# Dense products in half-array pairs, and one value phase per eight score steps, in an attention and gated-MLP block

## The chip, the cores and the metric

The kernel runs on one core of one Trainium2 chip. The metric is the device time of one execution in microseconds (us). TensorE (PE) multiplies, VectorE (DVE) and ScalarE (ACT) read its results from PSUM, GpSimd (POOL) works on SBUF alone, and SyncE (SP) issues nearly all DMA transfers. PEld is TensorE's loading of weights, which overlaps PE.

## The reference

One layer-normalised input of 2048 rows and 512 columns feeds two branches, attention with 32 heads of 16 and a gated MLP with a spatial product over the rows; both are added to the input. Everything is in fp32.

```python
def _A_ref(x, wqkv, wo):                     # attention, H = 32, Dh = 16
    q, k, v = ...                            # x @ wqkv, split by heads
    scores = jnp.einsum("bhqd,bhkd->bhqk", q, k) * (Dh ** -0.5)
    p = _softmax(scores, axis=-1)
    o = jnp.einsum("bhqk,bhkd->bhqd", p, v)
    return o.transpose(...).reshape(B, S, D) @ wo
def _B_ref(x, w_in, w_sp, b_sp, w_out):      # gated MLP, Fh = 896
    z = _gelu(jnp.einsum("bsd,df->bsf", x, w_in))
    z1, z2 = z[..., :Fh], _layernorm(z[..., Fh:], axis=-1)
    g = jnp.einsum("ts,bsf->btf", w_sp, z2) + b_sp[None, :, None]
    return jnp.einsum("bsf,fd->bsd", z1 * g, w_out)
xn = _layernorm(x, axis=-1)
return x + _A_ref(xn, A_wqkv, A_wo) + _B_ref(xn, B_w_in, B_w_sp, B_b_sp, B_w_out)
```

## The kernel before

**Attention.** Heads go in 16 pairs. A *score step* `scores(n)` (L840) makes one tile `st` of 128 keys by 512 queries for both heads of a pair: two matmuls of 50 rows (three parts of 16 and two rows that carry the negative maximum), one on the upper and one on the lower half of the array, into the two banks of one PSUM pair. There are 1024 steps. ACT takes the exponential of the whole pair into a buffer `pf` (L57). A *maximum step* `max_mm(m)` (L572) makes the same scores turned round, queries on partitions, again as two half-array matmuls (48 rows), and DVE reduces them (L580); there are 1024 of these too, and they run `LEAD` = 27 steps ahead. After every 16th, `max_fin` makes the row of maxima, which goes through DRAM into the two extra rows of `qst`. The *value products* `pv` (L814) take two `pf` buffers (two tiles of keys, two heads): four matmuls of 128 rows and 32 columns side by side, in fp32, which the chip does as two instructions each. They add up over 16 steps in the bank `o`, which ACT copies out. Three PSUM pairs (`s`) serve scores and maxima, one bank `o` the values and one bank `d` the dense products.

**Dense work.** All other products go through `mm3` (L167 to L169): both factors are split into a high and a low part, and three matmuls of 128 rows and up to 512 columns add up in the bank `d`. In this order: queries and keys of the later heads (`qk_rest`), the MLP's second half (`z2_all`) with its normalisation (`z2_norm`, mostly on POOL), its first half (`z1_all`), the spatial product (`spatial`, tile name `sp`), `mlp_out` (`mo`) and `attn_out` (`ao`). Each is a generator that yields after every three matmuls. Tiles finished in `d` are copied or added out by ACT or DVE; the splitting into high and low parts follows in generators of `side` and `bg`.

**Order.** The schedule is written out by hand when the kernel is built: the instructions of each engine stand in a fixed order, and semaphores do the rest. The main loop goes through *halves*, two for every three score steps. In an even half PE gets a score, a maximum, a score and then up to four half rounds of value products (`pv_some`); in an odd half a maximum, a score, a maximum and then dense work, as much as a credit allows that spreads it evenly up to step `DENSE` = 925. `later` and `flush` put DMA issues off by so many halves, and `prepare` brings weights in, through three buffers `raw` and POOL (L192, L193). Large tiles come from a ring of `RING` = 20 buffers: in the spatial stage 16 of them hold weights `wsp` and four hold pieces `zs` of z2, read back from DRAM at 512 KB each.

**Before the main loop** a prologue loads and normalises x, turns it round (`turn_x`), and makes queries and keys of the first group of heads (`qk_group(0, ...)`) and all values (`v_tile`).

Of the kernel before, what the change touches and what calls it, by code (L numbers as in the profile page):

```python
# [31 lines left out]
RING = 20  # L32
LEAD = 27
PF = 6
DENSE = 925
HALF = 2.7


@with_exitstack
def fused_block(ctx, tc, x, wqkv, wo, w_in, w_spT, b_sp, w_out, out):  # L40
# [5 lines left out]
    at = ctx.enter_context(tc.tile_pool(name="att", bufs=1))  # L46
# [6 lines left out]
    load = {"A": 0.0, "D": 0.0}  # L53

    def act(out, in_, func, n, **kw):
        load["A"] += 0.16 + n / 1400.0
        return nc.scalar.activation(out, in_, func, **kw)  # L57

    def dve(n, rate=1):
        load["D"] += 0.065 + n / (960.0 * rate)  # L60
        return nc.vector
# [35 lines left out]

    steady = []
    side = []
    left = [0]  # L100
# [6 lines left out]

    late = []  # L110
    now = [-2 * LEAD // 3 - 1]
# [3 lines left out]
    pool = [-1000.0]  # L115

    def clock():
        return HALF * now[0]

    def gps(us):  # L120
        pool[0] = max(pool[0], clock()) + us
        return nc.gpsimd

    def pool_done():
        t = pool[0]
        yield
        while clock() < t:
            yield

    def later(k, fn, *args):  # L130
        late.append((now[0] + k, fn, args))

    def flush():
        due = [l for l in late if l[0] <= now[0]]
        late[:] = [l for l in late if l[0] > now[0]]
        for _, fn, args in due:
            fn(*args)

    def store(dst, src, k=1):
        if steady:  # L140
            later(k, move, dst, src)
        else:
            nc.gpsimd.dma_start(raw(dst), raw(src))

    def piece(nm):
        return big.tile([P, 2, 512], F32R, tag="big", name=nm, bufs=RING)
# [7 lines left out]
    def dpsum(nm, tag="d", n=1):  # L154
        left[0] = n
        return ps.tile([P, 512], F32, tag=tag, name=nm, bufs=1)

    def spsum(nm):

        return ps.tile([P, 2, 512], F32, tag="s", name=nm, bufs=3)  # L160

    def split(dst_h, dst_l, src, n):
        act(dst_h, src, AF.Copy, n)
        dve(n).tensor_sub(dst_l, src, dst_h.bitcast(F32))
# [5 lines left out]

    rawfree = [-1000.0] * 3
# [24 lines left out]
    def prepare(out, loads, freed=None):  # L196


        loads, flight, made = list(loads), [], []
        while loads or flight or made:  # L200
            if made and clock() >= made[0][0]:
                _, k, t = made.pop(0)
                out[k] = t
            if flight and now[0] >= flight[0][0]:
                _, k, l = flight.pop(0)
                t = end(l)
                made.append((pool[0], k, t))
                rawfree.append(pool[0])
            if loads and len(rawfree) > 0 and clock() >= rawfree[0] and (freed is None or freed and now[0] >= freed[0]):
                rawfree.pop(0)  # L210
                if freed:
                    freed.pop(0)
                k, *a = loads.pop(0)
                flight.append((now[0] + 2, k, begin(*a)))
            yield

    wq, w2, w1, wsp, wout, wo_ = {}, {}, {}, {}, {}, {}
    bg = []
# [5 lines left out]
    def load_x(g):  # L224
        xt = [at.tile([P, 2, D], F32, tag="pf", name=f"x{g}_{i}", bufs=PF) for i in (0, 2)]
# [30 lines left out]
    def turn_x(g):  # L256
        for c in range(ND):
            pt = spsum(f"xT{g}_{c}")[:, 0, :]
# [3 lines left out]
            split(t[:, 0, :], t[:, 1, :], pt, 512)  # L262
# [16 lines left out]
    def qk_store(scr, order, hl, sl, first=False):  # L279
        put = move if first else store  # L280
        r = 1 if order[0] == order[1] else 0
        put(scr[:, r:r + 2, sl], hl)
        put(scr[:, 2 - 2 * r, sl], hl[:, 0, :])
# [4 lines left out]
    def qk_group(m, g, w, tags=("d",)):  # L288
        for a in range(2):
            if now[0] < -2 and m:  # L290
                tags = ("d", "o")
            acc = dpsum(f"qk{m}_{a}_{g}", tags[a % len(tags)], ND)
            for c in range(ND):
                t = xnT[g, c]
                mm3(acc, w[a][:, 0, c * P:(c + 1) * P], w[a][:, 1, c * P:(c + 1) * P], t[:, 0, :], t[:, 1, :], c == 0, c == ND - 1)
                yield 650 + 0.5 * (c == ND - 1)
            if m == 0:
                run(qk_split(m, g, a, acc))
                yield 0
                continue  # L300
            raw_ = t512(f"qr{m}_{a}_{g}")
            act(raw_, acc, AF.Copy, 512)
            side.append(qk_split(m, g, a, raw_))
            yield 0

    def qk_split(m, g, a, src):
        hl = hilo(f"qkhl{m}_{a}_{g}")
        act(hl[:, 0, :], src, AF.Copy, 512)
        yield
        dve(512).tensor_sub(hl[:, 1, :], src, hl[:, 0, :].bitcast(F32))  # L310
        qk_store((qscr, kscr)[a][m], ((0, 1, 0), (0, 0, 1))[a], hl, slice(g * 512, (g + 1) * 512), m == 0)
        yield

    def qk_prepare():
        yield from prepare(wq, [((m, a), *qk_weights(m, a)) for m in (2, 3) for a in range(2)])

    def qk_rest():
        for g in range(NG):
            for m in range(1, 4):
                if m == 3 and g + 1 < NG:  # L320
                    fetch_xnT(g + 1, 1 if now[0] >= 0 else 0)
                while (m, 1) not in wq:
                    yield -1.5
                if g == NG - 1 and m == 1:
                    bg.append(prepare(w2, [((c, j), f"w2_{c}_{j}", w_in[c * P:(c + 1) * P, FH + j * 448: FH + (j + 1) * 448], 448) for c in range(ND) for j in range(2)]))
                yield from qk_group(m, g, [wq[m, a] for a in range(2)])


    def v_tile(t, ws):
        acc = dpsum(f"v{t}", "do"[t % 2])  # L330
        sl = slice((t % 4) * P, (t % 4 + 1) * P)
        for c in range(ND):
            xt = xnT[t // 4, c]
            mm3(acc, xt[:, 0, sl], xt[:, 1, sl], ws[c][:, 0, :], ws[c][:, 1, :], c == 0, c == ND - 1)
        act(vhead[:, t, :, :DH], acc.rearrange("p (h d) -> p h d", d=DH), AF.Copy, 512)


    def gelu_in(x, u, n):

        gps(0.0022 * n).tensor_mul(u, x, x)  # L340
        gps(0.0011 * n).tensor_scalar(u, u, 0.044715, 1.0, ALU.mult, ALU.add)
        gps(0.0024 * n).tensor_mul(u, u, x)

    def gelu_out(x, u, n):

        dve(n).scalar_tensor_tensor(x, u, 1.0, x, ALU.add, ALU.mult)

    def z2_norm(t, z):


        z = z[:, :FH]
        u = piece(f"z2u{t}").bitcast(F32).rearrange("p a b -> p (a b)")[:, :FH]
        yield
        gelu_in(z, u, FH)
        yield from pool_done()
        act(u, u, AF.Tanh, FH, scale=GC)
        act(u, u, AF.Identity, FH, bias=1.0)
        yield
        gps(0.0024 * FH).tensor_mul(z, z, u)
        yield from pool_done()  # L360
# [3 lines left out]
        for j in range(2):  # L364
            dve(448).bn_stats(st[:, j, :], z[:, j * 448:(j + 1) * 448])
        dve(12).bn_aggr(mv, st)
        yield
        gps(0.2).tensor_scalar(rs[:, 0:1], mv[:, 1:2], 1.0, 4 * EPS, ALU.mult, ALU.add)
# [616 lines left out]
```

## Time and profile before

| | us |
|---|---|
| median of 3 runs (lowest, highest) | 1991.4 (1991.37, 1992.17) |
| profiled execution, its span | 1991.1 |
| PE busy | 1952.1 (98%) |
| DVE busy, of it the reduces of L580 | 1430.1 (72%), 1221.1 |
| ACT busy, of it the exponentials | 1244.0 (62%), 1027.6 |
| POOL busy | 521.0 (26%) |
| spatial stage, first to last matmul of `sp` | 691.4 to 1586.9 |

The profiled execution lasts as long as the runs. The granted clock of PE is 0.995 on average. A line of a group gives source line, engine, operation, tiles, shapes and count, then the busy time and the mean of one in ns, then the idle time before it and what ended it. A line of the timeline gives start, duration, engine, line, operation, tiles and how many instructions were merged. Ends of matmuls are modelled and overlap the next start, so a busy PE isn't a PE at its peak: what a matmul costs is read from the starts.

### The profile page before, as it was taken

The page shows a single profiled execution, that of the slowest core. Times are in us where ns is not written, and L with a number is a line of the kernel's source. Part 1 is how long each engine was busy: PE and PEld are TensorE (multiplying, and loading weights), DVE is VectorE, ACT ScalarE, POOL GpSimd, SP SyncE. Part 2 cuts the span into 40 slices and gives each one's busy share as a digit, 9 for nine tenths or more (in the row PEclk, how much of TensorE's full clock was granted, in tenths as well). Part 3 has the DMA queues.
Part 4 walks back from the last instruction along what each step waited for, and adds up shares of the span by engine and source line. Part 5 has one row for each costly group of instructions (what it writes and reads, how often), then busy time and mean ns, then how long its engine had stood idle before and what let it go on. Part 6 is the DMA issues. An engine that isn't in the chain of part 4 may idle for free.

```text
span 1991.1 us, 32474 instructions
## 1 busy us (share of the span) xinstructions
PE 1952.1 (98%) x12572; PEld 1056.2 (53%) x12572; DVE 1430.1 (72%) x1662; ACT 1244.0 (62%) x1412; POOL 521.0 (26%) x592
## 2 busy tenths in 40 slices
PE   7999999999999999999999999999999999999997
PEld 6765555554555555555555555555555555554553
DVE  5377677776788777777777777777777777777873
ACT  4337688887777665655565665565566655556665
POOL 3202167787454720005011420006001300011100
PEclk9999999998999999999999999999999999999999
DMA  9587344364533645355444745356365545344422
GB/s 327 187 301 229 101 125 118 99 145 143 137 112 130 186 144 133 92 150 165 128 143 146 211 134 139 92 129 191 108 157 155 167 132 140 128 139 137 125 79 86
DMA packets 233857, 293.18 MB, mean 147 GB/s; under 512 B 34656, under 2 KB 134688, under 8 KB 230824
## 3 DMA queue, kind: packets, MB, share of 16 engines
q1 hardware_dynamic: 229480, 281.07, 48.5%
q0 software_dynamic: 4224, 10.04, 1.4%
q8 instruction: 99, 1.62, 0.3%
q14 instruction: 54, 0.44, 0.1%
HBM read 189.06 MB, written 101.98 MB: 146 GB/s over the span
## 4 chain that ended last, share of the span: by engine, by line
PE 90%; DVE 4%; ACT 3%; DMA 2%; issue 1%; POOL 0%; SPq 0%; DVEq 0%; ACTq 0%; POOLq 0%
PE o L814 22%; PE mx L572 14%; PE st L840 14%; PE sp L167 6%; PE sp L169 5%; PE sp L168 5%; DVE mm L580 2%; PE mo L167 2%; PE qk L167 2%; PE z1p L167 2%; PE z2p L167 1%; PE qk L168 1%; PE qk L169 1%; ACT pf L57 1%; PE mo L169 1%; PE mo L168 1%
## 5 line engine op out<-in xcount | busy, mean ns | idle before, releaser
L580 DVE TENSOR_REDUCE mm<-mx 128x2 f32<-128x1024 f32 x1024 | 1221.1, 1222 | 467.9 <-PE mx L572 465.6
L57 ACT ACTIVATE pf<-st 128x1024 f32<-128x1024 f32 x1024 | 1027.6, 1024 | 634.9 <-PE st L840 610.1
L814 PE MATMUL o<-pf,vall 128*32 128x512 f32 (+1 forms) x5120 | 514.0, 515 | 0.0
L840 PE MATMUL st<-qst,kst 50*128 50x512 f32 x2048 | 446.5, 433 | 10.6 <-DVE mm L580 7.8
L572 PE MATMUL mx<-kst,qst 48*128 48x512 f32 x2048 | 448.6, 436 | 3.6 <-DVE mm L580 2.0
L572 PEld LDWEIGHTS mx<-kst,qst 48*128 48x128 f32 x2048 | 192.4, 185 | 272.7 <-ACT pf L57 177.4
L840 PEld LDWEIGHTS st<-qst,kst 50*128 50x128 f32 x2048 | 193.6, 185 | 175.1 <-issue 82.6
L814 PEld LDWEIGHTS o<-pf,vall 128*32 128x32 f32 x5120 | 131.8, 109 | 236.1 <-issue 212.4
L167 PE MATMUL sp<-wsp,zs 128*128 128x512 f32 x448 | 190.9, 426 | 0.0
L169 PE MATMUL sp<-wsp,zs 128*128 128x512 f32 x448 | 176.2, 393 | 0.0
L168 PE MATMUL sp<-wsp,zs 128*128 128x512 f32 x448 | 175.7, 392 | 0.0
L167 PEld LDWEIGHTS sp<-wsp,zs 128*128 128x128 f32 x448 | 83.9, 187 | 58.0 <-issue 43.6
L192 POOL CAST wsp<-wsp_0r 128x512 fp32r<-128x512 f32 x4 | 2.5, 615 | 363.2 <-DMA wsp_0r<-in_w_spT 363.2
L169 PEld LDWEIGHTS sp<-wsp,zs 128*128 128x128 f32 x448 | 84.1, 188 | 19.5
L168 PEld LDWEIGHTS sp<-wsp,zs 128*128 128x128 f32 x448 | 84.3, 188 | 13.7
L628 POOL TENSOR_TENSOR ob<-ob 128x512 f32<-128x512 f32 (+1 forms) x16 | 20.5, 1283 | 244.2 <-DMA ob<-escr 244.2
L633 POOL TENSOR_TENSOR ob<-ob 128x512 f32<-128x512 f32 (+1 forms) x16 | 21.0, 1312 | 144.7 <-DMA ob<-rscr 124.0
L167 PE MATMUL z2p<-w,xt 128*128 128x448 f32 x128 | 52.0, 406 | 0.0
L192 POOL CAST wo<-wo0r 128x512 fp32r<-128x512 f32 x1 | 0.6, 612 | 184.4 <-DMA wo0r<-in_wo 184.4
L167 PE MATMUL mo<-wout,hp 128*128 128x512 f32 x112 | 48.4, 432 | 0.1
L169 PE MATMUL z2p<-w,xt 128*128 128x448 f32 x128 | 47.5, 371 | 0.0
L168 PE MATMUL z2p<-w,xt 128*128 128x448 f32 x128 | 47.4, 370 | 0.0
(374 smaller groups left out, 1914.2 us busy)
## 6 DMA issues: line engine op xcount, KB each, us to landing
zs<-z2scr SPq DMA_DIRECT2D x112, 512.0 KB
escr<-e SPq DMA_DIRECT2D x60, 256.0 KB
hscr<-hhl SPq DMA_DIRECT2D x28, 512.0 KB
qst<-qscr SPq DMA_DIRECT2D x30, 384.0 KB
kst<-kscr SPq DMA_DIRECT2D x30, 384.0 KB
xscr<-xnT POOLq DMA_DIRECT2D x16, 512.0 KB, 6.0
qscr<-qkhl SPq DMA_DIRECT2D x16, 512.0 KB
kscr<-qkhl SPq DMA_DIRECT2D x16, 512.0 KB
```

The source lines that it names most:

```text
L57: return nc.scalar.activation(out, in_, func, **kw)
L167: nc.tensor.matmul(acc, lh, rh, start=first, stop=False)
L168: nc.tensor.matmul(acc, ll, rh, start=False, stop=False)
L169: nc.tensor.matmul(acc, lh, rl, start=False, stop=last)
L192: gps(0.6).tensor_copy(t[:, 0, :n], rw[:, :n])
L572: nc.tensor.matmul(acc[:, j, :], qst[p % 2][rows, tt * P:(tt + 1) * P], kst[p % 2][rows, kc * 512:(kc + 1) * 512], start=True, stop=True)
L580: dve(1024).tensor_reduce(mmax[i // 16][:, :, t, kc], mstep.pop(i), AX.X, ALU.max)
L628: gps(1.3).tensor_add(both[rows, 0, :], both[rows, 0, :], both[rows, 1, :])
L633: gps(1.3).tensor_mul(both[rows, 0, :], both[rows, 0, :], both[rows, 2, :])
L814: nc.tensor.matmul(acc[cols:cols + VW, a:a + w], vpack(kt - 1 + r, 2 * p + j), pf[:, j * 512 + a:j * 512 + a + w], start=(kt == 1 and a == ...
L840: nc.tensor.matmul(st[:, j, :], kst[p % 2][rows, kt * P:(kt + 1) * P], qst[p % 2][rows, c * 512:(c + 1) * 512], start=True, stop=True)
```

## The change

*Tiling of the dense products.* `dense` makes each product in 64-row halves: one slot holds two matmuls, the upper half of one operand pair into bank `banks[0]` and the lower half of another into `banks[1]`. `both` makes two output tiles x and y: first x's upper halves with y's lower halves, then, with the banks exchanged, y's upper with x's lower halves. Ahead of the exchange ("s") PE gets a drain, unless it has since waited for something that followed the last dense slot. In `spatial`, `mlp_out` and `attn_out` the tiles are paired in the same way, by loading the two halves of a piece from two tiles; the seventh tile of the spatial product is made as two half sums, which are added.

*Banks.* The dense products now have a pair of banks (`dps`), and the value products have none of their own: a value phase takes one of the three pairs of scores and maxima (`sl`), adds eight steps there, and is copied (first half of a chunk, ACT) or added (second half, DVE) into an SBUF tile `e`.

*Order.* The halves are replaced by a planner that keeps an estimated time for each engine (`T`) and takes, at PE's time, what can go next: a score or a maximum if a pair is free, by the shorter backlog of ACT and DVE; else a dense slot; and after `CYC` = 8 scores, when the dense generators have come to a pause ("q", after 21 to 24 slots) or have nothing ready, the value phase: four rounds in a row. Work of ACT, DVE and POOL is a set of generators that say engine and duration, and the planner lays them out by priority. Value products are no longer split into 256 columns.

*Moves.* Subtractions for low parts go from DVE to POOL (`qk_split`, `h_split`), as does the last step of z1's GELU; the squares of z2 go from POOL to ACT; the second tile of each pair is copied out by DVE (`qk_out`, `z2_out`, `z1_out`); weights are converted by ACT or POOL. `RING` is 18 (two pieces `zs` beside 16 weights), `PF` 7, and each piece `zs` is loaded by two transfers. Prologue and arithmetic are otherwise as they were.

```diff
-RING = 20
-LEAD = 27
-PF = 6
-DENSE = 925
+RING = 18
+LEAD = 24
+PF = 7
+CYC = 8
...
+    dps = ps.tile([P, 2, 512], F32, tag="d", name="dps", bufs=1)
+    sl = [ps.tile([P, 2, 512], F32, tag=f"s{i}", name=f"sl{i}", bufs=1) for i in range(3)]
...
+    def dense(n, a, b, banks=(0, 1), first=True, last=True, w=512):
+        for i in range(n):
+            slots = []
+            (ah, al, ar, as_), (bh, bl, br, bs) = a(i), b(i)
+            for k, (u, v) in enumerate((((ah, ar), (bh, br)), ((al, ar), (bl, br)), ((ah, as_), (bh, bs)))):
+                go, stop = first and i == 0 and k == 0, last and i == n - 1 and k == 2
+                slots.append([(banks[0], w, u[0][0:64], u[1][0:64], go, stop), (banks[1], w, v[0][64:128], v[1][64:128], go, stop)])
+            yield "t", slots
+
+    def both(n, x, y, w=512):
+        yield from dense(n, x, y, (0, 1), True, False, w)
+        yield "s",
+        yield from dense(n, y, x, (1, 0), False, True, w)
...
+            if swap and seen < lastd:
+                nc.tensor.drain()
...
+        def values():
+            p, c, kt0 = order[n_pv]
+            turn_to("V")
+            k = take("o")
+            for n in range(n_pv, n_pv + CYC, 2):
+                wait_for(lambda: n + 1 in ready and ready[n + 1] <= T["P"])
...
+                        nc.tensor.matmul(sl[k][cols:cols + VW, 0, :], vpack(kt + r, 2 * p + j), pf[:, j * 512:(j + 1) * 512], start=n == n_pv, stop=n == n_pv + CYC - 2)
...
+            if n_st - n_pv == CYC and free and n_pv + 1 in full:
+                more = mx_ok(t) and backlog("D", t) < 0.9
+                if not more and (hold or not has_dense(t)):
+                    values()
+                    continue
+            pick = []
+            if free:
+                if st_ok(t) and kind.count("s") < 2:
+                    pick.append((backlog("A", t), scores))
+                if mx_ok(t) and kind.count("m") < 2 and (n_st - n_pv < CYC or len(free) > 1 or backlog("D", t) < 0.9):
+                    pick.append((backlog("D", t) - 0.2, maxima))
+            if pick:
+                min(pick, key=lambda p: p[0])[1]()
+            elif has_dense(t):
+                dense_slot()
```

A group of maxima counts as ready 8.5 us after its last reduce (`maxready`), and no score is placed before that.

More of the change, by code (lines that the diff above doesn't have):

```diff
@@ L835, in scores @@
[L835 to L837 removed]
+        order = [(p, c, kt) for p in range(NP) for c in range(NG) for kt in range(NT)]
+        N = len(order)
+        slotfree = [0.0] * 3
+        pending = [0] * 3
+        kind = [""] * 3
+        full, ready, pfq = {}, {}, [0.0] * PF
+        parts = {}
+        slots = []
+        blocked = 0.0
+        swap = hold = False
+        pe = seen = lastd = 0
+        wrote = [0] * 3
+        stpos = {}
```

1174 lines of the change are left out of this document (674 added, 500 removed).

## The prediction

> **What bounds the kernel now.** I read the page first, for shares and counts, then the timeline of a few cycles in the longest stage, then the first and last starts by tile.
>
> ```profile
> span 1991.1 us, 32474 instructions
> PE 1952.1 (98%) x12572; PEld 1056.2 (53%) x12572; DVE 1430.1 (72%) x1662; ACT 1244.0 (62%) x1412; POOL 521.0 (26%) x592
> PE 90%; DVE 4%; ACT 3%; DMA 2%; issue 1%; POOL 0%; SPq 0%; DVEq 0%; ACTq 0%; POOLq 0%
> L580 DVE TENSOR_REDUCE mm<-mx 128x2 f32<-128x1024 f32 x1024 | 1221.1, 1222 | 467.9 <-PE mx L572 465.6
> ```
>
> PE is busy for 98% of the span and makes 90% of the chain that ended last. But a busy PE isn't a PE at its peak. Where its time goes is read from the spacing of matmul starts (second column: modelled duration, which overlaps the next start):
>
> ```profile
> 1002.38 2.36 DVE L580 TENSOR_REDUCE mm<-mx 128x2 f32<-128x1024 f32 x2
> ...
> 1003.06 0.39 PE L168 MATMUL sp<-wsp,zs 128*128 128x512 f32 x1
> 1003.07 0.19 PEld L169 LDWEIGHTS sp<-wsp,zs 128*128 128x128 f32 x1
> 1003.29 0.39 PE L169 MATMUL sp<-wsp,zs 128*128 128x512 f32 x1
> 1003.52 0.40 PE L167 MATMUL sp<-wsp,zs 128*128 128x512 f32 x1
> 1003.76 0.39 PE L168 MATMUL sp<-wsp,zs 128*128 128x512 f32 x1
> 1003.99 0.40 PE L169 MATMUL sp<-wsp,zs 128*128 128x512 f32 x1
> ...
> 1004.32 0.51 PE L840 MATMUL st<-qst,kst 50*128 50x512 f32 x2
> 1004.42 0.19 PEld L572 LDWEIGHTS mx<-kst,qst 48*128 48x128 f32 x2
> 1004.65 0.40 PE L572 MATMUL mx<-kst,qst 48*128 48x512 f32 x2
> 1004.89 0.40 PE L840 MATMUL st<-qst,kst 50*128 50x512 f32 x2
> 1004.92 2.06 ACT L57 ACTIVATE pf<-st 128x1024 f32<-128x1024 f32 x2 [1.22 <-PE st L840]
> 1005.10 1.23 DVE L580 TENSOR_REDUCE mm<-mx 128x2 f32<-128x1024 f32 x1 [0.36 <-PE mx L572]
> 1005.22 1.50 PE L814 MATMUL o<-pf,vall 128*32 128x256 f32 x16
> 1006.65 0.50 PE L572 MATMUL mx<-kst,qst 48*128 48x512 f32 x2
> 1006.99 0.40 PE L840 MATMUL st<-qst,kst 50*128 50x512 f32 x2
> 1007.22 0.41 PE L572 MATMUL mx<-kst,qst 48*128 48x512 f32 x2
> 1007.55 0.50 PE L167 MATMUL sp<-wsp,zs 128*128 128x512 f32 x1
> 1007.89 0.40 PE L168 MATMUL sp<-wsp,zs 128*128 128x512 f32 x1
> ...
> 1009.14 0.51 PE L840 MATMUL st<-qst,kst 50*128 50x512 f32 x2
> ```
>
> A cycle of three score steps goes from 1004.32 to 1009.14: 4.82 us. Three kinds of slot are in it. A dense matmul in the run from 1003.06 to 1003.99 takes 0.93/4 = 0.2325 us. A pair of half-array matmuls (st or mx, 50 and 48 rows, two at once) takes 0.24 (1004.65 to 1004.89) or 0.23 (1006.99 to 1007.22): 0.233. For the value products two stretches of another cycle give the price:
>
> ```profile
> 887.52 1.92 PE L814 MATMUL o<-pf,vall 128*32 128x512 f32 x16
> 889.38 0.50 PE L572 MATMUL mx<-kst,qst 48*128 48x512 f32 x2
> ```
>
> Two rounds (two keys' tiles, two heads each) take 1.86 with the way out, the one and a half from 1005.22 to 1006.65 take 1.43: half a round is 0.43, a round 0.86, and 0.14 is the way out. The cycle holds six half-array pairs, six dense matmuls and 1.5 rounds: 6 x 0.233 + 6 x 0.2325 + 1.29 = 4.08. The other 0.74 us are four changes of tiling: into o 0.33 instead of 0.233, out of o 0.14, and the second slot after each change is late (1006.65 to 1006.99: 0.34; 1007.55 to 1007.89: 0.34). That is 0.185 a change. With 1024/3 = 341 cycles they cost 341 x 0.74 = 252 us. This is the largest loss in the kernel, and the edit aims at it.
>
> **What the change does to PE.** First and last starts by tile:
>
> ```profile
> L572 PE MATMUL mx<-kst,qst x2048: 383/399/792, 87.7 to 1938.6; 48*128 48x512 f32 x187
> L719 PE MATMUL al<-sel,on x32: 587/624/692, 1944.4 to 1984.0; 32*128 32x512 f32 x32
> ```
>
> The prologue before 87.7 is left as it is, and so are the 7.1 us behind 1984.0. In between lie 1896 us. By the loops of the code they hold 2048 half-array pairs (477 us), 2496 dense matmuls of 512 columns and 28 for the bias (587), 384 of 448 columns (0.2325 x 448/512 = 0.203: 78), 512 rounds (0.86: 440), 252 us of changes and about 8 for the last pair of heads: 1842. PE thus idles some 54 us now.
>
> After:
> - *Dense work.* Every 128-row matmul becomes two of 64 rows, paired with two of another output tile: x's upper half with y's lower half, then, with the banks exchanged, the rest. Two tiles of n matmuls still take 2n slots. The trace has no long run of half-array pairs, and none that accumulates. Bounds for the slot: 0.23 (third of three pairs) and 0.34 (second after a change). I take 0.2325, as the pairs inside a triple are at 0.23 to 0.24 and a dense run is at 0.2325, both with LDWEIGHTS of 0.19. 12 bias slots fewer are 3 us.
> - *Changes.* Scores, maxima and dense share a tiling; only the value phase has another. Each of 128 cycles of eight steps pays once into o and once out of it: 0.10 + 0.14 + 0.105 = 0.34, so 44 us instead of 252: 208 saved.
> - *Drains.* One where banks are exchanged and PE hasn't waited since: in each of 12 qk, 16 z2, 14 z1 and 8 output pairs, and in a few spatial pairs, about 55. The trace shows none. A change of tiling (0.185) bounds it below, a whole matmul plus a restart (0.39 + 0.1) above: 10 to 27 us; I take 0.25, as it resembles the change, so 14. Behind a drain stand all later slots, scores too; ACT and DVE have a tile of 1.0 and 1.2 us in hand meanwhile.
> - *Sum without idle time:* 87.7 + 477 + 584 + 78 + 440 + 44 + 14 + 8 + 7 = 1740.
>
> [...]
>
> **Idle time after.** Per cycle with a dense stretch of 24 slots (the generators pause after that many): 16 x 0.233 + 24 x 0.2325 + 3.44 + 0.34 + 0.11 = 13.2 us of PE. DVE needs eight maxima at 2.36/2 = 1.18: 9.4. It also has a hole around the value phase: 3.44 + 0.34, plus 0.45 from a pair's start to its reduce (1004.65 to 1005.10), less two maxima waiting (2.36), 1.9 us. The evacuations of dense tiles, now half on DVE, and the adding of the second half phase are issued just there and fill it. 11.3 us: PE stays the bound. ACT needs eight exponentials at about 1.0. Three places remain:
> 1. There are about 122 dense stretches. From the first maximum to the first score pass 16 x 1.18 + 0.9 + the planner's 8.5 = 28 us (1.18 from the reduce rows, 8.5 from the code). Less some 20 maxima of 0.233 that is 23 us of PE, four stretches of 5.6. 118 are left for 128 cycles. The ten without one last 11.3 us with 7.5 of PE work: 10 x 3.8 = 38.
> 2. The z2 stage is tight on everything:
>
> ```profile
> L359 POOL TENSOR_TENSOR z<-z,z2u 128x896 f32<-128x896 f32 x16 | 33.7, 2108 | 14.5 <-ACT z2u L57 12.3 <-DMA z2scr<-z2hl 2.2
> L57 ACT ACTIVATE z2u<-z2u 128x896 f32<-128x896 f32 x32 | 30.5, 954 | 0.5
> L384 POOL TENSOR_TENSOR z2hl<-z,z2hl 128x512 fp32r<-128x512 f32 (+1 forms) x32 | 36.9, 1152 | 16.7 <-ACT z2hl L57 16.7
> L341 POOL TENSOR_SCALAR z2u<-z2u 128x896 f32<-128x896 f32 x16 | 15.1, 943 | 1.4
> L365 DVE BATCH_NORM_STATS2 zst<-z 128x6 f32<-128x448 f32 x32 | 18.3, 613 | 0.0
> L57 ACT ACTIVATE z2hl<-z 128x512 fp32r<-128x512 f32 (+1 forms) x32 | 18.6, 582 | 0.0
> L57 ACT ACTIVATE z<-z2p 128x448 f32<-128x448 f32 x32 | 17.5, 546 | 0.0
> ```
>
> A tile costs POOL 2 x 2.11 + 2 x 0.94 + 2 x 1.15 = 8.4 and a dozen smaller ones, which I put at 3. ACT needs eight exponentials (8), 2 x 0.95, 2 x 0.58 and 0.55: 11.6. DVE needs 11.3 plus at least one bn_stats: 12. PE needs 12.5. I put 1 us of waiting on each of 16: 16.
> 3. The lead-in and the gaps between dense units there (one pair of banks, copied out before the next unit starts): about 12.
>
> 38 + 16 + 12 = 66, so 1740 + 66 = **1806 us** in the profiled execution. It took 1991.1 before and the median of the runs is 1991.4, so no correction: -9.3%.
>
> Of the moved steps: subtractions go from DVE to POOL (52 of them, 1.152 x 512/448 = 1.32 each by the z2hl row, on an engine busy 26%). SP gets two transfers for each spatial piece instead of one, and only two pieces of lead instead of four. Its queue is in order, so a late semaphore there delays pieces behind it:
>
> ```profile
> 90.00:150.00 60.00, 57.38 (x251) 38.55 (x250) 42.46 (x48) 22.40 (x35) 9.39 (x12) 1.00 0.75 267
> 691.00:1600.00 909.00, 906.19 (x5970) 477.01 (x5966) 670.00 (x745) 547.09 (x580) 154.29 (x156) 1.00 0.52 145
> ```
>
> The last two columns are DMA share and GB/s. The spatial stage has 56 stretches x 13.2 = 740 us instead of 909, so the same bytes raise the share from 0.52 to 0.64, below the 0.75 under which the lead-in still ran. If each of its 112 pieces came 0.5 us late, that would be 56 us: in the range, not in the sum.
>
> **Rivals.**
> - *The slots couple the engines (0.12).* Scores, maxima and the value accumulator now share three PSUM pairs. One is held 0.45 + 1.02 + about 0.2 by a score and 0.45 + 1.22 + 0.2 by a maximum: 3.54/3 = 1.18 us a step if PE always refills at once. If it doesn't, the value phase (3.8), its copy (0.6, by the z2p row) and the restart (0.45) simply stand behind eight steps: 14.3 us x 128 + 87.7 + 28 + 7 = **1953**. For: DVE and PE are both near full. Against: only six maxima per cycle must fit between value phases.
> - *PE can't issue so fast (0.04).* A dense slot becomes four instructions in 0.2325 us instead of two. Two value rounds show 32 in 1.72 us, 0.054 each, and the cycle above 68 in 4.82, 0.071: the limit is below that. At the middle, 0.0625, a slot would be 0.25 (4928 x 0.0175 = 86) and a round of 16 instructions 1.0 (512 x 0.14 = 72): 1806 + 158, less some 34 of idle time absorbed, **1930**. [...] Against a limit:
>
> ```profile
> 1981.33 0.38 PEld L706 LDWEIGHTS nd<-e,sel 128*32 128x32 f32 x16 [1.61 <-ACT e L57]
> 1981.33 0.65 PE L706 MATMUL nd<-e,sel 128*32 128x128 f32 x16 [0.70 <-ACT e L57]
> ```
>
> 32 instructions within 0.65 us, though in a short burst.
> - *Slower: a run of accumulating halves doesn't stream (0.09).* If two row tiles that add into two banks ran at the 0.34 of the second slot above, 2880 x 0.105 = 302 us more: **2108**. It loses to the kernel before from a slot of 0.2325 + 185/2880 = 0.297 on. For: no row shows such a run. Against: triples of pairs, and 128-row matmuls adding into one bank.
> - *The tiling isn't one (0.02).* If pairs of 48, 50 and 64 rows were different tilings, scores strewn among dense slots would make some 20 changes a cycle: 118 x 20 x 0.185 = 437, so 2240. Against: mx (48) to st (50) costs nothing, 1004.65 to 1004.89.
>
> **How the numbers follow.** Forecast 0.73: 1806, alone 1740 (no idle time, cheap drains) to 1890 (late pieces 56, drains 13, slot 0.235). Up to 1945 takes in the sequencer and half of the slots' case; what is left out is the rest of it, the two slow cases and the forecast's own tails, about 2 in 10. Faster by over 0.2% (about what a measurement can tell from no change): 0.73 + 0.12 + 0.04, less 0.02 of the slots' case, 0.87. Slower: 0.09 + 0.02 + 0.01 of that case, 0.12. Same 0.01.
>
> **What would show it.** Right: dense pairs 0.23 apart in runs; one o stretch of about 3.8 us every 13 us; spatial stage near 740 us; first mx near 88. Wrong: pairs at 0.3 or more; mx or st waiting on ACT and DVE in every cycle; POOL or DMA ending PE's waits in the z2 or spatial stage.

## Result: 1.7% slower, and the profile after

| | before | after |
|---|---|---|
| median of the runs (lowest, highest), us | 1991.4 (1990.9, 1992.2) | 2027.3 (2023.5, 2031.1) |
| profiled execution, its span, us | 1991.1 | 2023.5 |
| granted clock of PE, mean | 0.995 | 0.960 |
| PE busy | 1952.1 (98%) | 1871.4 (92%) |

The ratio of after to before is 1.0174, 95% interval 1.0156 to 1.0191. The forecast was 1806, range 1740 to 1945: time and sign are wrong. Lines of the page of after:

```profile
span 2023.5 us, 37561 instructions
PE 1871.4 (92%) x14428; PEld 1105.9 (55%) x14428; DVE 1443.2 (71%) x1677; ACT 1254.3 (62%) x1393; POOL 629.1 (31%) x701
PEclk9999999999999999999999899999999999878997
L754 DVE TENSOR_REDUCE mm<-sl 128x2 f32<-128x1024 f32 x1024 | 1218.3, 1223 | 288.4 <-PE sl L1044 267.9
```

PE is busy for less time, yet the end is later, and no other engine has filled up. Something makes PE wait, in many places, and the clock line isn't all nines any more. First the part that did what it should, in the timeline of one cycle of the spatial stage (PE alone; start, modelled duration, how many instructions were merged):

```profile
1000.47 0.40 PE L1044 MATMUL sl<-kst,qst 48*128 48x512 f32 x2
1000.70 0.88 PE L1088 MATMUL dps<-wsp,zs 64*128 64x512 f32 x6
1001.41 0.40 PE L1030 MATMUL sl<-qst,kst 50*128 50x512 f32 x2
1001.65 0.40 PE L1088 MATMUL dps<-wsp,zs 64*128 64x512 f32 x2
1001.89 0.39 PE L1044 MATMUL sl<-kst,qst 48*128 48x512 f32 x2
...
1005.41 0.62 PE L1088 MATMUL dps<-wsp,zs 64*128 64x512 f32 x4
1005.96 3.64 PE L1111 MATMUL sl<-pf,vall 128*32 128x512 f32 x32
1009.53 0.50 PE L1044 MATMUL sl<-kst,qst 48*128 48x512 f32 x2
...
1013.94 0.79 PE L1088 MATMUL dps<-wsp,zs 64*128 64x512 f32 x1 [3.66 <-DMA zs<-z2scr]
```

Three dense slots go from 1000.70 to 1001.41: 0.237 each. One slot goes from 1001.65 to 1001.89: 0.24, with a score ahead and a maximum behind. So accumulating halves stream, and scores among them cost no change of tiling. The value phase with its way out takes 3.57 (1005.96 to 1009.53). The last line shows one thing that went wrong: a piece `zs` is late, and PE stands 3.66 us.

Where the time is, by stage, from the same trace. A cycle reaches from the start of one value phase to the start of the next, and cycles are numbered from 0; the forecast by the prediction's own prices is 13.2, in the z2 stage 13.5 (12.5 and 1 of waiting), without dense work 11.3.

| part | cycles | mean us | forecast | above forecast, us | at half clock, us |
|---|---|---|---|---|---|
| up to the first maximum | | 114.2 | 87.7 | 26.5 | 0 |
| first maximum to first score (the lead) | | 39.7 | 28 | 11.7 | 5 |
| queries and keys | 8 | 13.83 | 13.2 | 5 | 2 |
| z2 | 16 | 14.98 | 13.5 | 24 | 17 |
| z1 | 14 | 14.91 | 13.2 | 24 | 10 |
| spatial | 56 | 14.41 | 13.2 | 68 | 34 |
| mlp_out | 16 | 13.86 | 13.2 | 11 | 7 |
| no dense work, middle | 6 | 15.10 | 11.3 | 23 | 48 |
| attn_out | 8 | 15.49 | 13.2 | 18 | 6 |
| last four, no dense work | 4 | 12.38 | 11.3 | 4 | 21 |

These are 215 of the 217 us between 1806 and 2023.5. Half the clock was granted for 163 us in all, 22 in the kernel before (here and below the last spell is counted whole, 2 us past the end of the span).

The windows of the same stages (from and to, length, busy us and count of PE, PEld, DVE, ACT and POOL, then clock, DMA share, GB/s) put nearly half of the half clock where PE has little to do: the third line is the stretch without dense work, the fourth the end.

```profile
275.00:514.00 239.00, 222.75 (x1790) 135.30 (x1782) 186.17 (x235) 184.10 (x215) 172.99 (x231) 0.96 0.45 121
723.00:1530.00 807.00, 775.14 (x6302) 468.05 (x6302) 597.46 (x667) 504.06 (x534) 175.30 (x165) 0.98 0.59 154
1752.00:1842.00 90.00, 81.13 (x384) 28.03 (x384) 62.65 (x70) 50.34 (x51) 2.53 (x2) 0.74 0.22 55
1966.00:2023.50 57.50, 39.18 (x260) 12.56 (x256) 18.29 (x24) 25.75 (x28) 0.00 (x0) 0.76 0.15 56
```

### The profile page after: what moved, and what is told of

Read it like the earlier page. It is cut to its first block, busy times and chain, and to the rows that moved or that the text cites. A ratio compares the mean times of both kernels' runs of the same rounds, so it can differ in the third digit from the quotient of the medians.

```text
span 2023.5 us, 37561 instructions
## 1 busy us (share of the span) xinstructions
PE 1871.4 (92%) x14428; PEld 1105.9 (55%) x14428; DVE 1443.2 (71%) x1677; ACT 1254.3 (62%) x1393; POOL 629.1 (31%) x701
## 5 line engine op out<-in xcount | busy, mean ns | idle before, releaser
L754 DVE TENSOR_REDUCE mm<-sl 128x2 f32<-128x1024 f32 x1024 | 1218.3, 1223 | 288.4 <-PE sl L1044 267.9
L63 ACT ACTIVATE pf<-sl 128x1024 f32<-128x1024 f32 x1024 | 1043.0, 1026 | 486.9 <-PE sl L1030 301.0
L1111 PE MATMUL sl<-pf,vall 128*32 128x512 f32 x4096 | 501.9, 625 | 20.4 <-ACT pf L63 12.9
L1044 PE MATMUL sl<-kst,qst 48*128 48x512 f32 x2048 | 444.5, 423 | 30.8 <-ACT pf L63 15.3
L1030 PE MATMUL sl<-qst,kst 50*128 50x512 f32 x2048 | 445.2, 426 | 27.0 <-DVE mm L754 18.2
L1088 PE MATMUL dps<-wsp,zs 64*128 64x512 f32 x2688 | 436.5, 399 | 19.5 <-DMA zs<-z2scr 18.7
L1088 PEld LDWEIGHTS dps<-wsp,zs 64*128 64x128 f32 x2688 | 271.7, 190 | 68.5 <-DMA zs<-z2scr 16.8
L1030 PEld LDWEIGHTS sl<-qst,kst 50*128 50x128 f32 x2048 | 202.6, 189 | 193.8 <-DVE mm L754 87.1
L1111 PEld LDWEIGHTS sl<-pf,vall 128*32 128x32 f32 x4096 | 127.7, 114 | 322.7 <-issue 258.9
L1044 PEld LDWEIGHTS sl<-kst,qst 48*128 48x128 f32 x2048 | 200.7, 188 | 185.5 <-ACT pf L63 76.4
L1088 PEld LDWEIGHTS dps<-wout,hp 64*128 64x128 f32 x672 | 65.6, 189 | 10.2
```

Of the source, the lines that this page charges most:

```text
L754: nc.vector.tensor_reduce(mmax[g][:, :, t, kc], sl[k], AX.X, ALU.max)
L1030: nc.tensor.matmul(sl[k][:, j, :], kst[p % 2][rows, kt * P:(kt + 1) * P], qst[p % 2][rows, c * 512:(c + 1) * 512], start=True, stop=True)
L1044: nc.tensor.matmul(sl[k][:, j, :], qst[p % 2][rows, tt * P:(tt + 1) * P], kst[p % 2][rows, kc * 512:(kc + 1) * 512], start=True, stop=True)
L1088: nc.tensor.matmul(dps[:, bank, :w], lhs, rhs, start=go, stop=stop)
L1111: nc.tensor.matmul(sl[k][cols:cols + VW, 0, :], vpack(kt + r, 2 * p + j), pf[:, j * 512:(j + 1) * 512], start=n == n_pv, stop=n == n_pv + ...
```

## The experiments

Four theories on the 217 us: (1) the prologue waits on two banks of one tile; (2) the clock is halved where PE's work is thin; (3) late transfers hold up engines that work in order; (4) the planner's order leaves too little slack, so that delays add up instead of being absorbed. The rivals are in the expectations. Every kernel is the changed one with the edit shown. Ratios are to the kernel before, measured beside each run; its median was 1991.4 to 1995.2 us, so that differences between runs of different sessions are good to some 4 us.

**Prologue on two pairs of banks (e1_prologue).**

```diff
-        return sl[turns[0] % 3]
+        return sl[turns[0] % 2]
-            acc = dps[:, a, :]
+            acc = (dps, sl[2])[a][:, 0, :]
-        acc = dps[:, t % 2, :]
+        acc = (dps, sl[2])[t % 2][:, 0, :]
```

> In the changed kernel the first maximum starts at 114.2 us instead of 87.7. Here the prologue's products alternate between the dense pair and one of the three slot pairs, two tiles instead of the two banks of one tile; the transposes rotate over the other two. Theory (each product of the prologue waits until the other bank of the same tile has been copied out): the first maximum is back at 88 to 92, the whole 22 to 27 us shorter, about 2002. Rival (the prologue is longer because of the smaller ring of buffers or its transfers): first maximum stays near 114 and the time near 2027.

Measured: 1998.7, ratio 1.0029 [1.0008, 1.0051]; 28.6 us of 2027.3 gone. First of after, on the prologue's timeline, then of this run, on the groups of the tile `sl` (first and last start):

```profile
64.72 0.39 PE L221 MATMUL dps<-kst,xnT 128*128 128x512 f32 x1
65.80 0.50 PE L219 MATMUL dps<-xnT,wqk 128*128 128x512 f32 x1 [0.69 <-ACT vall L63]
...
68.42 0.39 PE L221 MATMUL dps<-xnT,wqk 128*128 128x512 f32 x1
70.27 0.50 PE L219 MATMUL dps<-xnT,wqk 128*128 128x512 f32 x1 [1.46 <-DVE qkhl L216]
```

```profile
L1044 PE MATMUL sl<-kst,qst x2048: 386/395/793, 89.7 to 1947.2; 48*128 48x512 f32 x187
```

In after a product into one bank starts only when the copy of the other bank is done: 0.69 and 1.46 us of waiting in these lines, 20.0 in the 20 such waits of the prologue (11.7 for copies `qkhl`, 8.3 for `vall`); in this run no product of the prologue waits for them. With banks of two tiles the first maximum is at 89.7, as before (87.7). Theory 1 stands: 24.5 of the 26.5 us up to the first maximum are gone, and the whole gains no less.

**Dummy products where PE would wait (e2_warm).** Pairs of 64-row, 256-column products into `dps` while it is idle:

```diff
+            elif n_pv < N and dfree[0] <= t and not filling:
+                turn_to("R")
+                for bank, r in enumerate((slice(0, 64), slice(64, 128))):
+                    nc.tensor.matmul(dps[:, bank, 0:256], dummy[r, 0:P], dummy[r, :], start=True, stop=True)
+                T["P"] += SLOT
+                pe += 1
+                lastd = pe
```

> Adds useless half-array pairs of 256 columns into the idle dense banks wherever the planner has nothing for PE and no dense product is open; the output is not touched. Theory (PE's clock is halved when the work gets thin, and the value phase at half clock lengthens cycles that ACT and DVE bound): half-clock time falls from 163 us to under 80, the six cycles without dense work from 15.1 to 11.5-12.5, the z2 cycles from 15.0 to about 14.3, the whole 25 to 40 us shorter, about 1992. Rival (the halved clock is a symptom, the cycle is set by the round trips of ACT and DVE): the clock is restored, the cycles stay near 15 and the time within 8 us of 2027.

Measured: 2025.9, ratio 1.0159 [1.0142, 1.0176]. Half clock falls from 163 to 80 us. Cycles without dense work go from 15.10 to 13.59, z2 from 14.98 to 14.45, the last four from 12.38 to 10.95: 23 us together. But `mlp_out` loses 17, `attn_out` 8, and the first score comes 3.5 later. After's stretch without dense work, the same window in this run:

```profile
1752.00:1842.00 90.00, 87.36 (x796) 53.26 (x794) 70.41 (x78) 57.24 (x59) 4.80 (x4) 1.00 0.27 72
```

The clock is 1.00 instead of 0.74, and DVE gets 70.4 us of work done in 90 instead of 62.7. The price of a spell is read best in z2, where all cycles of both kernels hold eight maxima. Starts of value phases, after first, then this run:

```profile
346.45 5.34 PE L1111 MATMUL sl<-pf,vall 128*32 128x512 f32 x32 [0.38 <-DVE mm L754]
362.63 3.64 PE L1111 MATMUL sl<-pf,vall 128*32 128x512 f32 x32
377.32 1.38 PE L1111 MATMUL sl<-pf,vall 128*32 128x512 f32 x8 [0.38 <-DVE mm L754]
```

```profile
349.45 3.64 PE L1117 MATMUL sl<-pf,vall 128*32 128x512 f32 x32
363.92 3.64 PE L1117 MATMUL sl<-pf,vall 128*32 128x512 f32 x32
378.64 1.06 PE L1117 MATMUL sl<-pf,vall 128*32 128x512 f32 x8
```

In after the first of the two cycles holds a spell of 3.4 us at half clock and lasts 16.18, here 14.47; the second holds none and lasts 14.69 and 14.72. Five such spells in z2 are the 8.5 us gained there. So the clock is a cause in its stages. The edit does more than raise it, though: a dummy pair moves the planner's time on by `SLOT` (0.23 us) where it otherwise steps 0.05, so the order of the useful work changes too. After has no cycle of more than nine maxima in `mlp_out`; here two hold ten and last 16.4 and 16.6, and one at the head of `attn_out` holds twelve and lasts 18.8. In another (cycle 95, 19.0) PE waits 3.80 for the row of maxima (`qst<-mscr`). That is where part of the gain went.

A cycle without dense work at full clock also shows what such a cycle really costs (DVE first, then PE):

```profile
1789.02 2.46 DVE L757 TENSOR_REDUCE mm<-sl 128x2 f32<-128x1024 f32 x2
1794.54 2.36 DVE L757 TENSOR_REDUCE mm<-sl 128x2 f32<-128x1024 f32 x2 [3.06 <-PE sl L1048]
```

```profile
1790.42 3.64 PE L1117 MATMUL sl<-pf,vall 128*32 128x512 f32 x32
1803.80 1.07 PE L1117 MATMUL sl<-pf,vall 128*32 128x512 f32 x8
```

It lasts 13.38 us, with 3.06 in which DVE has no maximum, and the end of a group of maxima (0.8) in it.

**Weights loaded earlier, output normalised later (e3_patience).** `LOAD` is how far ahead of its conversion a transfer is planned; the waits of the normalisation of the attention output are the others.

```diff
-LOAD = 5.0
+LOAD = 8.0
-        yield "T", 10.0
+        yield "T", 16.0
-        yield "T", 8.0
+        yield "T", 14.0
```

> The planner counts 8 us instead of 5 until a weight has landed, and 16 and 14 instead of 10 and 8 in the normalisation of the attention output. Theory (conversions and copies are put on ACT and POOL before their transfer has landed, and the exponentials stand behind them): the stalls of 5 to 9 us in cycles 26, 52, 65, 66, 118 and 120 shrink, 15 to 35 us shorter, about 2000. Rival (weights only come later, and the dense work waits instead): 2020 to 2045.

Measured: 2000.1, ratio 1.0042 [1.0026, 1.0057], 27 less than after. In the spatial stage the longest cycles with late weights are gone (numbers 52, 65, 66 and 81, which took 18.7 to 22.9 us); 26 still lasts 19.4, and 58 and 90 stay; `attn_out` gets worse, 17.45 a cycle.

**One 128-row matmul for each dense slot (e4_fullrow).** The count of slots is as in after, and a part of the products is not the reference's.

```diff
-                slots.append([(banks[0], w, u[0][0:64], u[1][0:64], go, stop), (banks[1], w, v[0][64:128], v[1][64:128], go, stop)])
+                x, bank = (v, banks[1]) if k == 1 else (u, banks[0])
+                slots.append([(bank, w, x[0], x[1], first and i == 0 and k < 2, last and i == n - 1 and k > 0)])
```

> Each dense slot is one matmul of 128 rows in place of two of 64, into the two banks by turns; all else, the order too, is as in the changed kernel. Where a piece holds halves of two tiles the products are not the reference's, so only the time counts. Theory (the common tiling is what makes scattered scores cheap): some 2680 changes between half-array and 128-row slots at 0.19 us, 510 us, of which at most 230 go into idle time: 2300 to 2530. Rival (tiling costs nothing, slots are what matters): 2010 to 2040.

Measured in one run: 2442.0, 415 above after. Its timeline in the spatial stage:

```profile
1207.41 0.40 PE L1045 MATMUL sl<-kst,qst 48*128 48x512 f32 x2
1207.74 0.97 PE L1089 MATMUL dps<-wsp,zs 128*128 128x512 f32 x3
1208.64 0.49 PE L1031 MATMUL sl<-qst,kst 50*128 50x512 f32 x2
1209.06 0.50 PE L1089 MATMUL dps<-wsp,zs 128*128 128x512 f32 x1
1209.49 0.50 PE L1045 MATMUL sl<-kst,qst 48*128 48x512 f32 x2
```

A lone slot between scores now takes 0.43 (1208.64 to 1209.06, 1209.06 to 1209.49) where after has 0.24. The common tiling is what makes the strewn scores cheap: the change's main idea holds.

**Several at once (e5_stalls, e6_paced, e7_paced_warm).** e5: the prologue of e1, `LOAD` 8 and longer waits of the normalisation for the first three groups. e6: the same with shorter dense stretches in part of the spatial stage, so that dense work lasts longer (its main line is shown last). e7: e6 with the dummies.

```diff
-        yield "T", 4.0
+        yield "T", 4.0 if g4 == 3 else 16.0
-        yield "T", 10.0
+        yield "T", 10.0 if g4 == 3 else 16.0
-        yield "T", 8.0
+        yield "T", 8.0 if g4 == 3 else 14.0
...
-                if s == 7:
+                if s in (((6, 13) if opens else (4, 11)) if paced else (7,)):
```

> Prologue in two tiles (as e1), 8 us until a weight is taken as landed (as e3), and the normalisation of the attention output counts 16, 16 and 14 us for the first three groups only, so that its loads come after those of the next heads' rows; the last group keeps 4, 10 and 8. Theory (the stalls of 5 to 9 us come from bursts of transfers and from work queued on ACT ahead of its data): cycles 26, 58 and 90 shrink from 20-25 us to under 17, no new wait in the output product, and with the 27 us of the prologue the whole is about 1960 (1950 to 1972), less than the kernel before. Rival (stalls only move): 1990 to 2005, the sum of the prologue's gain and nothing else.

> As e5_stalls, and in two of three pairs of the spatial product dense work pauses after every 7 key tiles instead of 8, so that the same slots fill some eight more cycles. Theory A (a cycle without dense work is lost time): the six empty cycles go, each worth 15.1 - 13.2 plus its 5.5 us of missing dense work spread elsewhere, 10 to 35 us below e5_stalls. Theory B (a cycle can't be shorter than about 13.2 us by the hole that the value phase tears into DVE's work, 3 us, and 8 maxima): shortened spatial cycles stay at 13 us, and the whole is within 12 us of e5_stalls.

> As e6_paced, with the useless pairs of e2_warm in PE's idle time. Theory (clock): z2 cycles 0.5 us shorter each and the tail 6 us, so 8 to 18 us below e6_paced. Rival (useless pairs delay what comes next as much as the clock gives): within 8 us of it or above.

Measured: 2014.1 (ratio 1.0105 [1.0078, 1.0132]), 2024.5 (1.0154 [1.013, 1.0178]) and 2009.3 (1.0072 [1.0047, 1.0097]). e5 missed both its ranges: cycles 26, 58 and 90 fall below 17 as expected, but others grow long instead, and `attn_out` costs 18.05 a cycle. e6 has no cycle without dense work in the middle, but 65 spatial cycles of 14.6: more evenness gained nothing here. e7 against e6 has 52 us less at half clock and gains 15. That isn't the clock alone: the z2 cycles, which gain 17, hold 6 to 12 maxima in e6 (the one with twelve lasts 19.9) and eight or nine in e7.

**Fuller thresholds (e8_fuller, e9_full_only, e10_full_load8, e11_full_warm).** The planner may place a maximum ahead of a value phase while DVE's backlog is below 1.6 instead of 0.9 us. e8 is e5 with this, e9 e1 with this, e10 e9 with `LOAD` 8, e11 e8 with the dummies.

```diff
-                more = mx_ok(t) and backlog("D", t) < 0.9
+                more = mx_ok(t) and backlog("D", t) < 1.6
...
-                if mx_ok(t) and kind.count("m") < 2 and (n_st - n_pv < CYC or len(free) > 1 or backlog("D", t) < 0.9):
+                if mx_ok(t) and kind.count("m") < 2 and (n_st - n_pv < CYC or len(free) > 1 or backlog("D", t) < 1.6):
```

> As e5_stalls, but the value phase starts only when DVE has at least 1.6 us of maxima ahead (0.9 before), so that it idles less in the phase. Theory (DVE's hole of 3 us in each value phase sets the cycles without or with short dense work): DVE's wait per value phase falls from about 3.0 to 2.2 us, the odd spatial cycles stay at 12.9, z2 and empty cycles are 0.3 to 0.8 us shorter, the whole 5 to 25 us below e5_stalls. Rival (PE then waits for DVE before the phase): equal or up to 25 us above it.

> Prologue on two pairs of banks and the fuller thresholds (1.6 for 0.9), nothing else. Theory A, the thresholds alone make the planner's order robust: e8 was 46 us below e5 by them, so this is about 45 below the 1998.7 of e1: 1940 to 1965. Theory B, they only mend what the longer patience and the deeper loading lead of e5 had spoilt (e5 was 15 above e1): then 1985 to 2005, as e1.

> The same with the transfers of weights planned 8 us instead of 5 ahead, the waits of the normalisation as in the changed kernel. If late weights are what stretches the cycles in the spatial stage, 5 to 15 us below the kernel with the thresholds alone; if the planner's order only shifts, within 8 us of it either way. The attention output should cost 16 us a cycle or less, as the normalisation isn't put off: 1940 to 1965 in all.

> e8 with dummy products where PE would wait, as in e2. e8 has 108 us of half clock. Theory clock: the half clock falls to below 70 and the total by 10 to 15 us, as between e6 and e7: 1953 to 1959. Rival, the dummies delay what they precede as in e2: 1965 to 1975, with the half clock lower all the same.

Measured: e8 1968.5 (ratio 0.987 [0.9841, 0.99]), e9 2032.5 (1.0201 [1.0186, 1.0216]), e10 1994.4 (1.0009 [0.999, 1.0029]), e11 1957.9 (0.9821 [0.9799, 0.9842]). The thresholds gain 46 over e5 and lose 34 against e1: both theories of e9 missed, and so did e10, 38 below e9 and 29 above its range. In the 5 us behind the start of a value phase DVE idles 2.64 us on average in e8, 2.63 in e5, so the hole that was to shrink did not. e11 came out as the clock theory had it (11 gained, half clock 108 to 45 us). It is the cleanest of the pairs with dummies: the z2 cycles hold the same counts of maxima as in e8, and the five of six maxima that hold a spell in e8 fall from about 14.1 to 12.6.

**Weights loaded earlier, alone (e12_load8_only), with dummies (e13_load8_warm), earlier still (e14_load12_warm).** e12 is e1 with `LOAD` 8; e13 adds the dummies; e14 has `LOAD` 12.

> Prologue on two pairs of banks and the transfers of weights planned 8 us ahead, nothing else: one half of e3 without its longer waits of the normalisation. Theory A, e3 gained by the earlier transfers: the 27 us of e3 come on top of the 27 of e1, so 1965 to 1980, with the long cycles near the conversions of weights gone. Theory B, it gained by the longer waits: 1990 to 2005, as e1. Theory C, effects of such small settings don't add up, as each moves the whole order behind it: anything from 1980 to 2030, with long cycles at other places than in e1 and e3.

> e12 with dummy products where PE would wait. Theory clock: e12 has 156 us of half clock; as between e6 and e7 (52 us less, 15 us gained) and between e8 and e11 (63 less, 11 gained) it falls to below 90 and the total by 10 to 20: 1953 to 1963. Rival, the dummies only delay what they precede, as the sum of e2 came out: 1968 to 1978.

> The same with the transfers of weights planned 12 us ahead instead of 8. Theory A, late transfers still stretch cycles: 10 to 25 us below e13. Theory B, eight were enough, and what is left is thin or uneven work of the cycles: within 6 us of e13. Theory C, the later release of tiles makes cycles without dense work again: above e13 by over 6 us.

Measured: e12 1973.1 (ratio 0.9884 [0.9862, 0.9906]), e13 1945.0 (0.9753 [0.9733, 0.9773]), e14 1963.4 (0.9841 [0.9805, 0.9877]). e12 hits theory A: `LOAD` alone gives 25.6 us, about the 27 that e3 had, on top of the 28.6 of e1. Waits of ACT on the transfers of the spatial weights (sum, times, longest), the three largest in e1 and then all in e12:

```profile
ACT wsp L63 <- DMA wsp_12r<-in_w_spT: 11.3, 2, 6.1
ACT wsp L63 <- DMA wsp_1r<-in_w_spT: 4.8, 2, 3.6
ACT wsp L63 <- DMA wsp_2r<-in_w_spT: 3.7, 2, 2.1
```

```profile
ACT wsp L63 <- DMA wsp_13r<-in_w_spT: 3.1, 1, 3.1
ACT wsp L63 <- DMA wsp_14r<-in_w_spT: 1.2, 1, 1.2
```

In e12 spatial cycles 52, 66 and 67 of e1 (22.2, 24.3 and 18.7 us) are ordinary; the stage and the middle stretch without dense work, 62 cycles in both, take 865.5 instead of 896.6. The order changed elsewhere too: the lead is 7 shorter, z2 12 longer.

e13 is the fastest kernel of the study, 2.5% below the one before and 28 us below e12, more than the 10 to 20 expected. Lines of its page:

```profile
span 1945.5 us, 38427 instructions
PE 1842.7 (95%) x14856; PEld 1119.6 (58%) x14856; DVE 1441.6 (74%) x1677; ACT 1247.9 (64%) x1383; POOL 635.0 (33%) x712
```

Half clock falls from 156 to 56 us, z2 from 15.73 to 14.59 a cycle, the last four cycles from 12.41 to 10.95. Of the 18 us gained in z2 the clock is again only a part: there e12 has one cycle of twelve maxima (20.1 us) and others of six to ten, e13 has eight or nine in each. e14 is 18 slower than e13, the side of theory C but not its mechanism: in the middle no cycle is without dense work. The spatial work is spread over 66 cycles instead of 60, and a cycle gets no shorter by that (13.96 and 13.94); the four short ones at the end, without maxima, are gone.

## Why the prediction was wrong

**Right.** *Dense work:* slots at 0.23 to 0.24, two matmuls each. The rival that a run of accumulating halves doesn't stream is refuted (three slots at 0.237 us each), and so is the one that PE can't issue so fast, the range's case of the sequencer: it had 1.0 for a round of value products, and four with the way out take 3.57. The loads of the weights don't come on top: those of the slot at 1001.65 start at 1001.42, 0.19 long, under the score of 1001.41, and from that score to the slot pass 0.24. *Changes:* paid twice per eight steps; e4 shows that the common tiling is the reason (0.43 us for a lone slot, 0.24 in after). *Stretches:* 122, ten cycles without dense work, as counted. Of the 0.74 us of changes in a cycle before, the prediction names 0.45; the rest stands in the lines that it shows (0.33 instead of 0.233 from 1003.99 to 1004.32, from there to 1004.65, and from 1007.22 to 1007.55), so the sum holds. The saving of PE work is real; it was lost to waiting.

What failed is the time in which PE stands idle: 66 us were put down for it, and the profiled execution lasts 283 us beyond the 1740 without idle time.

**Wrong, step by step.**

1. "The prologue before 87.7 is left as it is", and the description of the change says the same. It wasn't: a tile of values went by turns into the banks `d` and `o`, which are two tiles, and now goes by turns into the two banks of `dps`, which is one. That is the 26.5 us, of which e1 takes 24.5. The edit that moved the banks was read for its main use alone.
2. "11.3 us: PE stays the bound." A cycle without dense work and with eight maxima costs 13.0 to 13.4 at full clock (e2): in the one shown the hole of DVE is 3.06, not 1.9, because DVE has about one maximum and not two in hand when the value phase starts (1.06 us of work at 1790.42). Eight maxima (1218.3/1024 = 1.19 each, 9.5), the hole, half a group's end (0.4) and half an addition of values (0.35) make DVE's side 13.3, as long as PE's 13.2 in a cycle with dense work. Nor does each cycle hold eight: of after's 56 spatial cycles 27 hold seven maxima and 26 nine, mostly by turns, and undisturbed they last 12.9 and 13.9 to 14.1. One of nine, whose value phases start at 1412.87 and 1426.93 (DVE):

```profile
1412.52 1.23 DVE L754 TENSOR_REDUCE mm<-sl 128x2 f32<-128x1024 f32 x1
1416.98 3.54 DVE L754 TENSOR_REDUCE mm<-sl 128x2 f32<-128x1024 f32 x3 [3.24 <-PE sl L1044]
```

   Nine maxima (10.7) and the hole of 3.24 are 13.9: here DVE is the bound, with dense work and at full clock. That there is no slack, so that whatever delays either engine lengthens the cycle, is argued from this. It is half of the first rival (the slots couple the engines, 14.3 a cycle), which had a chance of 0.12. After's mean cycle, 14.5, is near that 14.3 by luck: it is made of cycles of 12.9 to 13.9 and of long ones that wait for transfers or run at half clock.
3. Nothing was said of the clock. Of each of after's six cycles without dense work in the middle 8 us are at half clock, which is why they last 15.1; five in z2 have 3.4 us of it. A value phase in that middle stretch of after (PE; it is longer than the 3.64 above, and so are the scores and maxima ahead of it):

```profile
1778.31 0.69 PE L1044 MATMUL sl<-kst,qst 48*128 48x512 f32 x2
...
1780.40 0.79 PE L1030 MATMUL sl<-qst,kst 50*128 50x512 f32 x2
1781.12 5.16 PE L1111 MATMUL sl<-pf,vall 128*32 128x512 f32 x32
```

   A spell of 3.4 us costs a z2 cycle 1.5 us (against its neighbours in after) to 1.7 (against the same cycle of e2). e6 to e7, e8 to e11 and e12 to e13 gain 15, 11 and 28 us with work that computes nothing, but that work moves the planner's order too, so these sums are not the price of the clock alone; how much of the 28 is order, no run separates.

4. "If each of its 112 pieces came 0.5 us late": in the range only, and the real mechanism is different. Few transfers hold up an engine, for 3 to 7 us, and it stands with all that its order has behind. Six of the 56 spatial cycles (52, 58, 65, 66, 81 and 90, 18.7 to 22.9 us) hold 45 of that stage's 68 us above the forecast, and cycle 26 holds 12 of z1's 24. Cycle 26 (25.2 us) in after:

```profile
543.00 1.30 SPq L115 DMA_DIRECT2D os<-escr  x2
544.35 1.65 SPq L115 DMA_DIRECT2D ob<-escr  x2
546.10 0.40 SPq L115 DMA_DIRECT2D z2scr<-z2hl  x1
...
553.36 0.71 ACT L63 ACTIVATE z2hl<-z,zrs 128x384 fp32r<-128x384 f32 x1 [6.54 <-DMA z2scr<-z2hl]
553.98 0.57 ACT L63 ACTIVATE e<-sl 128x512 f32<-128x512 f32 x1
554.61 0.80 PE L1044 MATMUL sl<-kst,qst 48*128 48x512 f32 x2 [6.77 <-ACT e L63]
```

   ACT waits 6.54 for a buffer that is still being stored; behind it in its order stands the copy of the value phase, and PE waits 6.77 for that. In cycle 52 it is a weight whose conversion the change gave to ACT:

```profile
934.85 0.63 ACT L63 ACTIVATE wsp<-wsp_12r 128x512 fp32r<-128x512 f32 x1 [4.83 <-DMA wsp_12r<-in_w_spT]
936.44 0.80 PE L1044 MATMUL sl<-kst,qst 48*128 48x512 f32 x2 [4.95 <-ACT pf L63]
```

   With the weights planned earlier (e12) cycles 52, 66 and 67 of e1 are ordinary and the whole gains 26 us; as the order changed with it, not all of that need be the weights. Cycles 58 and 90 wait for `zs` or stand in the burst of loads for the attention output, and stay long even in e13 (21.0 and 21.2). Of the 11.7 us of the lead e12 takes 6 (first maximum 90.3, first score 123.8); the rest is open.
5. "I put 1 us of waiting on each of 16" in z2: 14.98 instead of 13.5 a cycle. With dummies 14.45 to 14.6, so about a third is the clock; what makes the rest isn't settled.
6. Drains: 59 of them. In after one lies between the starts at 214.24 and 214.75 (0.51 instead of 0.24), and the next slot takes 0.33: about 0.4 in all where 0.25 was forecast; 59 x 0.15 is 9 us.

The sum of e13 is 139 above the forecast still; by its cycles, spatial (60 x 0.74 = 44), z1 (22), z2 (17) and `attn_out` (20) hold most. Open stays why the planner's small settings don't add up: the fuller thresholds are worth -46, +34 and +21 us (on e5, e1 and e12), the longer waits +41 without them (e5 against e12) and -26 with them (e8 against e10). The traces show that long cycles turn up at other places each time, and that the maxima are spread over the cycles in other ways (eight each in z2 of after, six and ten by turns in e8, six to twelve in e12); they don't show a rule. That the kernel has no slack to absorb a shifted instruction (step 2) fits, but is only argued.

## What to carry to other kernels

When PE work is taken out, work out the next engine's time per cycle with its hole, not only its busy time, and look at how its work is spread over the cycles: 13.3 beside 13.2 is two bounds, and a cycle with one maximum more is over both. Follow each buffer that a change moves into all of its users, the prologue among them, and look for instructions that wait for a DMA ahead of work that PE needs in the order of the same engine (the 4.83 us in which ACT waited for a weight kept PE waiting 4.95); planning those transfers 3 us earlier was worth 26 us here. Watch the granted clock where PE's work has become thin: here a spell of 3.4 us at half clock cost a cycle 1.5 to 1.7 us, and products that nobody reads brought the time at half clock from 163 to 80 us (e2). Where a planner lays out the order, such an edit changes the order as well, so compare cycles of the same work before a gain is put down to the clock.

## What the hardware showed

- In after the granted clock falls to 0.50 in 26 spells: 25 of 3.4, 6.8 or 10.2 us, and one at the end of the record. Six of them begin between 1752 and 1842 (mean clock 0.74), where the longest wait of PE between modelled ends is 0.5 us. The waits of that window (sum, times, longest):

```profile
PE sl L1030 <- DVE mm L754: 6.7, 19, 0.5
PE sl L1044 <- ACT pf L63: 0.8, 3, 0.3
```

- Two banks of one PSUM tile held each other up here: 65.80 and 70.27 above wait 0.69 and 1.46 us for copies out of the other bank. With two tiles the waits are gone, and the first maximum starts at 89.7 instead of 114.2 (e1). Whether hardware or the program's tracking of tiles does it, no run separates.
- Lone 128-row slots between half-array pairs take 0.43 us, 64-row pairs 0.24 (e4 and after).
